# Attention, expert layer and MLP on one core: inputs laid out in chunks on the host, scores on halves of the array's rows, scalings on GpSimd

## The chip, the cores and the metric

The kernel runs on one core of one Trainium2 chip. The metric is the device time of one execution in microseconds (us).

## The reference

Three stages follow each other. The attention is a retention: scores are multiplied by a causal decay, without a softmax. Its output is the input of a layer that gives each token to one of eight experts, with a capacity, and the result goes through an MLP with x * sigmoid(1.702 x).

```python
# q, k, v: (4, 8, 576, 64) = batch, heads, positions, width; float32
scores = scale * np.matmul(q, k.transpose(0, 1, 3, 2))
gamma = 1.0 - 2.0 ** (-5.0 - np.arange(H))
Dmat = np.where(rel >= 0, gamma[:, None, None] ** rel[None, :, :], 0.0)
x = np.matmul(scores * Dmat[None], v)            # then to (2304, 512)
# experts: 8, w1 (8, 512, 1024), w2 (8, 1024, 512)
expert_idx = np.argmax(x @ w_gate, axis=1)       # weight: that expert's softmax
h = np.maximum(np.einsum('ecd,edf->ecf', disp, w1), 0.0)
y = np.einsum('ecf,efd->ecd', h, w2)             # rows back to their tokens, by weight
# MLP: w_in (512, 2048), w_out (2048, 512), given as float64
h = x @ w_in
g = h * (1.0 / (1.0 + np.exp(-1.702 * h)))
out = g @ w_out
```

## The kernel before

The change lies in the attention stage, the first 150 us. Its work is cut into 20 chunks (`NT`): each of the four batch rows has four chunks of 128 positions and one of 64 (`NC = 5`, `CH`). One chunk holds all eight heads, two of them beside each other in the 128 partitions, so that four pairs (`NP = 4`) make a tile of 128 x 4 x 128.

The decay gamma^(i-j) is split in a factor for the query's position (table `gq`) and one for the value's (`gv`); what is left for the scores is a causal mask (`mk`). The table `gq` is loaded for the first chunk of a batch row and scaled up by `scales(c)` on ScalarE (L303) for the others.

These functions emit the work of chunk n:

- `load(n)` (L261): three loads on SyncE's queue, of queries, keys and values, as rows of positions. Each head's 64 numbers are a piece of 256 bytes in the source (L268).
- `emit_T(n)` (L308): TensorE transposes the queries (L315) and keys (L321) in four pieces each. VectorE multiplies the turned queries by the decay on the way out of PSUM (L317); ScalarE copies the turned keys into `kz` (L324), a pair of tiles in which the rows of the other head of a pair are zeros.
- `emit_V(n)` (L326): VectorE multiplies the values by their decay (L331).
- `emit_SC(n)` (L334): eight score products, each over all 128 rows of the array, with `kz` as weights (L342). VectorE multiplies by the mask (L344).
- `emit_KV(n)` (L348): eight products of keys and values (L357) add up the state of a batch row; ScalarE copies it to `St` (L361). Each product fills one half of the array's columns.
- `emit_XO(n)` (L363): the output, from the state of the earlier chunks (L369) and the chunk's own scores (L372, by halves of the array's columns).
- `emit_XR(n)` (L377): the output of chunk n once more as rows and the routing scores of its tokens (L383), then three small steps on VectorE (L392 to L394).
- `emit_EX(n)`, `emit_ST(n)` (L397, L407): the weight of the chosen expert, and the weighted rows, stored in `xd`.
- `gate1`, `gate2`, `gate3`: for groups of chunks (`GROUPS`), lists of the tokens of each expert, mostly on VectorE.

An fp32 product or transpose in the program may be more than one instruction: the eight products of L342 are sixteen instructions of the trace.

The order is written out by hand in the loop over chunks (L555 to L595), and each engine works through its instructions in that order. Iteration n loads chunk n+4, turns chunk n+2, forms the scores of chunk n+1 and the output of chunk n, and the routing scores of chunk n-1:

```python
            load(n + 4)
            if n > 1:
                emit_T(n + 2)
            if n > 1:
                emit_ST(n - 2)
            emit_SC(n + 1)
            emit_XO(n)
            emit_KV(n + 1)
            if n:
                emit_XR(n - 1)
            emit_V(n + 2)
```

Other work is put between. The MLP's weights come as float64 and are rounded to float32 by `convert` (L204) in pieces of six VectorE steps (L216 to L224), with a load and, for some, a store on SyncE's queue. `pad()` puts such steps between VectorE's work for a chunk: `FILL_A` gives the number for each chunk of a batch row, `CONV_A` the pieces done in the attention stage, and `FILL_C` the number of steps by expert and step in the experts' stage, where the rest of them goes. GpSimd sets the tile `yh` to zero at the start (L290) and is then idle until it gathers the tokens of the first expert (L646). The first weights of an expert are loaded on SyncE's queue in the last iterations.

Of the kernel before, what the change touches and what calls it, by code (L numbers as in the profile page):

```python
# [11 lines left out]
F32 = mybir.dt.float32  # L12
# [10 lines left out]
P = 128  # L23
# [8 lines left out]
ZROW = N  # L32
GW = P + E
WR = [370, 344, 324, 314, 304, 294, 288, 278]
W = max(WR)
NB = N // P + E
# [8 lines left out]
CONV_A = 10  # L45
FILL_A = [4, 2, 4, 4, 4]
FILL_C = [0, 3, 3, 3, 3, 3, 3, 2]
# [7 lines left out]
def _consts():  # L55
    """Tables that depend on the shapes alone."""
# [10 lines left out]
    tri = (i[:, None] < i[None, :]).astype(np.float64)  # L67
# [10 lines left out]
    parts = [("ident", np.eye(P)), ("gq", gq), ("causal", causal), ("gv", gv), ("gs", gs), ("tri", tri),  # L78
# [16 lines left out]
def fused(ctx: ExitStack, tc, q, k, v, wg, w1, w2, cap, w_in, w_out, cf, out):  # L95
# [14 lines left out]
    # tables and state that live through the kernel  # L110
# [42 lines left out]
    def load_w(r, i):  # L153
        """An eighth of the weights for a place."""
# [20 lines left out]
    # ------------------------------------------------------------ float64 weights to float32  # L175
# [28 lines left out]
    def convert(lo, hi):  # L204
        """Rounds pieces of the weights to the nearest float32, from the words of the float64; an operation at a time."""
# [27 lines left out]
    # ------------------------------------------------------------ attention and routing  # L233
    with ExitStack() as a:
# [14 lines left out]
        tri_f = acst.tile([P, P], F32, name="tri_f")  # L249
        tri = acst.tile([P, P], BF16, name="tri")  # L250
        one = acst.tile([P, P], BF16, name="one")
        kz = [acst.tile([P, 2, NP, P], F32, name=f"kz{i}") for i in range(2)]
        St = [acst.tile([P, NP, P], F32, name=f"St{i}") for i in range(3)]

        qr, kr, vr = {}, {}, {}
# [5 lines left out]
        def load(n, *between):  # L261
            if n >= NT:
                return
            b, c = divmod(n, NC)
            C = CH[c]
            for nm, src, dst, bufs in (("q", q, qr, 3), ("k", k, kr, 4), ("v", v, vr, 5)):
                t = rows.tile([P, H, D], F32, tag=nm, name=nm, bufs=bufs)
                nc.sync.dma_start(t[:C], src[b, :, c * P:c * P + C, :].rearrange("h p d -> p h d"))  # L268
                dst[n] = t
                for f in between[:1]:  # L270
                    f()
                between = between[1:]

        load(0, lambda: (nc.sync.dma_start(ident, cc("ident")),
                         nc.sync.dma_start(gs, cc("gs").rearrange("p (c a) -> p c a", a=NP)),
                         nc.sync.dma_start(gq[:, 0], cc("gq").rearrange("p (a i) -> p a i", i=P))),
             lambda: nc.sync.dma_start(mk, cc("causal")))
        nc.sync.dma_start(gv, cc("gv").rearrange("p (c h) -> p c h", h=H))
        load(1)
        nc.sync.dma_start(iw[:, :, P:], wg.rearrange("(k p) e -> p k e", p=P))  # L280
        load(2)
        for i in range(2):
            nc.vector.memset(kz[i], 0.0)
# [6 lines left out]
        nc.gpsimd.memset(yh.bitcast(F32), 0.0)  # L290
        nc.gpsimd.dma_start(xd[ZROW:ZROW + 1, :], yh[0:1, 0, :DM].bitcast(F32))
# [13 lines left out]
        qT, at_t, xT_t, lg_t, kv_t, xr_t = {}, {}, {}, {}, {}, {}  # L305
# [20 lines left out]
        def emit_V(n):  # L326
            if n >= NT:
                return
# [719 lines left out]
```

## Time and profile before

| | us |
|---|---|
| median of 3 runs | 801.19 (798.92 to 801.2) |
| span of the profiled execution | 799.6 |
| TensorE busy | 768.2 (96%) |
| VectorE busy | 525.6 (66%) |
| ScalarE busy | 371.7 (46%) |
| GpSimd busy | 63.7 (8%) |

The profile is of one execution of its own, and its page gives the span from the first to the last instruction, 799.6 us. The busy shares are means over three stages with different limits: attention to about 150 us, the experts to about 505 us, then the MLP. PE is TensorE's products, PEld its loads of weights, DVE is VectorE, ACT ScalarE, POOL GpSimd and SP SyncE. Matmul ends are modelled, so the start of one group of products and the start of the next is a safer measure than the durations.

### The profile page before, as it was taken

How to read it: one execution, taken by the hardware profiler on the slowest of the kernel's cores; microseconds unless marked ns; L12 is line 12 of the kernel's file. 1: busy time of each engine (PE TensorE's matmuls, PEld its weight loads, DVE VectorE, ACT ScalarE, POOL GpSimd, SP SyncE). 2: the span in 40 equal slices, each digit the busy share in tenths (PEclk: the TensorE clock that was granted, in tenths of full speed). 3: DMA queues.
4: the chain of work that ended last, by engine and by line, in shares of the span. 5: the costliest groups of instructions: out<-in, count | busy, mean ns of one | idle time of the engine just before them, and what ended most of it. 6: DMA issues, size and time to landing. Idle time of an engine off the chain costs nothing.

```text
span 799.6 us, 13741 instructions
## 1 busy us (share of the span) xinstructions
PE 768.2 (96%) x5072; PEld 707.1 (88%) x5072; DVE 525.6 (66%) x1285; ACT 371.7 (46%) x788; POOL 63.7 (8%) x71
## 2 busy tenths in 40 slices
PE   6999996699999999999999999999999999999995
PEld 5899996689999999999999999999999988888884
DVE  3587888576787888898798888744434345343442
ACT  3655554336555566566544444444333344343432
POOL 5000000701011011000000000030000003000003
PEclk9999999699999999999999999999999999999998
DMA  9889858435576576675522222020000002000002
GB/s 196 193 195 223 199 126 282 128 107 181 175 251 199 195 245 204 195 268 169 202 67 66 67 67 66 1 80 1 1 0 1 1 1 80 0 1 1 1 1 82
DMA packets 94295, 90.26 MB, mean 113 GB/s; under 512 B 61719, under 2 KB 67223, under 8 KB 94224
## 3 DMA queue, kind: packets, MB, share of 16 engines
q1 hardware_dynamic: 77200, 45.90, 21.7%
q10 hardware_dynamic: 13312, 33.56, 13.1%
q0 software_dynamic: 3712, 9.88, 3.6%
q8 instruction: 42, 0.69, 0.4%
q14 instruction: 29, 0.24, 0.1%
HBM read 75.15 MB, written 14.16 MB: 112 GB/s over the span
## 4 chain that ended last, share of the span: by engine, by line
PE 60%; issue 31%; DVE 3%; POOL 2%; DMA 2%; ACT 1%; SPq 0%; POOLq 0%; ACTq 0%
PE h L674 14%; PE acc L693 13%; PE h L846 9%; PE y L871 8%; PE sc L342 4%; PE xr L383 2%; PE xo L372 2%; POOL out L884 2%; PE xo L369 2%; PE tx L654 1%; PE kv L357 1%; PE pk L321 1%; PE pq L315 1%; DMA xg<-xd,IDX 1%; DMA k<-in_k 0%
## 5 line engine op out<-in xcount | busy, mean ns | idle before, releaser
L852 DVE TENSOR_TENSOR sg<-h,sg 128x384 f32<-128x384 f32 (+1 forms) x96 | 53.5, 557 | 131.0 <-ACT sg L851 131.0
L851 ACT ACTIVATE sg<-h 128x384 f32<-128x384 f32 (+1 forms) x96 | 47.3, 492 | 165.1 <-PE h L846 163.9
L871 PE MATMUL y<-b,gh 128*128 128x512 f32 x288 | 112.4, 390 | 0.0
L871 PE MATMUL y<-a,gl 128*128 128x512 f32 x288 | 112.3, 390 | 0.0
L871 PE MATMUL y<-a,gh 128*128 128x512 f32 x288 | 112.2, 389 | 0.0
L625 DVE TENSOR_TENSOR b<-w1r,a 128x512 fp32r<-128x512 f32 x112 | 77.2, 689 | 14.8 <-ACT a L624 14.4
L846 PE MATMUL h<-yh,b 128*128 128x384 f32 (+2 forms) x384 | 82.7, 337 | 0.0
L846 PE MATMUL h<-yh,a 128*128 128x384 f32 (+2 forms) x384 | 82.7, 337 | 0.0
L846 PE MATMUL h<-yl,a 128*128 128x384 f32 (+2 forms) x384 | 82.6, 337 | 0.0
L854 ACT CAST gh<-sg 128x384 fp32r<-128x384 f32 (+1 forms) x96 | 49.3, 513 | 71.2 <-DVE sg L852 70.6
L693 PE MATMUL acc<-hi,a 128*128 128x370 f32 (+7 forms) x256 | 80.1, 313 | 0.0
L855 DVE TENSOR_TENSOR gl<-sg,gh 128x384 fp32r<-128x384 f32 (+1 forms) x96 | 53.6, 558 | 38.9 <-ACT gh L854 31.3
L693 PE MATMUL acc<-lo,a 128*128 128x370 f32 (+7 forms) x256 | 78.8, 308 | 0.0
L693 PE MATMUL acc<-hi,b 128*128 128x370 f32 (+7 forms) x256 | 78.8, 308 | 0.0
L634 DVE TENSOR_TENSOR b<-w2r,a 128x512 fp32r<-128x512 f32 x112 | 76.8, 685 | 1.8 <-ACT a L633 1.1
L633 ACT CAST a<-w2r 128x512 fp32r<-128x512 f32 x112 | 69.0, 616 | 17.7 <-PE acc L693 16.8
L846 PEld LDWEIGHTS h<-yh,a 128*128 128x128 f32 x384 | 68.2, 188 | 9.1 <-ACT yh L698 0.2
L624 ACT CAST a<-w1r 128x512 fp32r<-128x512 f32 x112 | 69.2, 618 | 12.6 <-issue 3.7
L846 PEld LDWEIGHTS h<-yh,b 128*128 128x128 f32 x384 | 66.4, 188 | 2.7
L846 PEld LDWEIGHTS h<-yl,a 128*128 128x128 f32 x384 | 66.1, 188 | 2.8
L871 PEld LDWEIGHTS y<-a,gl 128*128 128x128 f32 x288 | 54.1, 188 | 11.5
L871 PEld LDWEIGHTS y<-a,gh 128*128 128x128 f32 x288 | 54.1, 188 | 8.6
(157 smaller groups left out, 1305.0 us busy)
## 6 DMA issues: line engine op xcount, KB each, us to landing
w1r<-in_moe_w ACTq DMA_DIRECT2D x28, 512.0 KB, 4.4
w2r<-in_moe_w ACTq DMA_DIRECT2D x28, 512.0 KB, 3.6
cs<-in_moe_w_in SPq DMA_DIRECT2D x32, 256.0 KB, 3.2
cs<-in_moe_w_out SPq DMA_DIRECT2D x32, 256.0 KB, 2.7
q<-in_q SPq DMA_DIRECT2D x16, 256.0 KB, 3.9
k<-in_k SPq DMA_DIRECT2D x16, 256.0 KB, 4.6
v<-in_v SPq DMA_DIRECT2D x16, 256.0 KB, 4.8
xd<-xrow SPq DMA_DIRECT2D x16, 256.0 KB, 2.5
```

The lines of the kernel that those rows point to most:

```text
L624: nc.scalar.copy(a, s)
L625: nc.vector.tensor_tensor(b, s, a, op=ALU.subtract)
L633: nc.scalar.copy(a, s)
L634: nc.vector.tensor_tensor(b, s, a, op=ALU.subtract)
L674: nc.tensor.matmul(h[:, :n], wt[:, kc, :], xs[e, kc][j][:, :n], start=i == 0, stop=i == 3 * KC - 1)
L693: nc.tensor.matmul(y[dc][:, :n], wt[:, dc * P:(dc + 1) * P], x[:, :n], start=fc == 0 and i == 0, stop=fc == NF - 1 and i == 2)
L846: nc.tensor.matmul(h[:, :n], wt[:, kc, :], x[:, kc, o:o + n], start=i == 0, stop=i == 3 * KC - 1)
L851: nc.scalar.activation(sg[:, :n], h[:, :n], AF.Sigmoid, scale=1.702)
L852: nc.vector.tensor_tensor(sg[:, :n], h[:, :n], sg[:, :n], op=ALU.mult)
L854: nc.scalar.copy(gh[:, :n], sg[:, :n])
L855: nc.vector.tensor_tensor(gl[:, :n], sg[:, :n], gh[:, :n], op=ALU.subtract)
L871: nc.tensor.matmul(accs[bi][c // P + t], x[:, t * P:(t + 1) * P], wt, start=f == 0 and i == 0, stop=f == 2 * NF - 1 and i == 2)
```

## The change

Queries, keys and values are laid out by chunks before the launch (`_chunks`). `in_qk` has for each chunk 128 partitions with the queries and then the keys, already turned; `in_kv` has the keys and values as rows of positions. So `load(n)` is two loads, each with up to 4 KB in one piece for a partition, and the keys are loaded in both forms. The transposes, their evacuations, `kz` and its zeros go. Queries and values are multiplied by their decays in place, by `emit_Q(n)`, on GpSimd, and on VectorE for chunk 0 alone. Each score product uses 64 rows of the array, the upper or lower half, for one head of a pair.

Smaller parts: the products of the state (`emit_KV`) stand inside `emit_XO`, between the two kinds of output products, whose order is exchanged. All `scales` are made ahead of the loop. The zeros of `yh` are set in eight slices, in iterations 2 to 9. The table `tri` is made from two others. Six pieces of weights instead of ten are converted in the attention stage, two steps in each of iterations 2 to 17; the four others are added in the experts' stage.

```diff
+YW = (N + WR[1]) // 2
-CONV_A = 10
-FILL_A = [4, 2, 4, 4, 4]
-FILL_C = [0, 3, 3, 3, 3, 3, 3, 2]
+CONV_A = 6
+FILL_A = [2, 2, 2, 2, 2]
+FILL_C = [0, 3, 3, 3, 3, 4, 4, 3]
...
         def load(n, *between):
...
-            for nm, src, dst, bufs in (("q", q, qr, 3), ("k", k, kr, 4), ("v", v, vr, 5)):
-                t = rows.tile([P, H, D], F32, tag=nm, name=nm, bufs=bufs)
-                nc.sync.dma_start(t[:C], src[b, :, c * P:c * P + C, :].rearrange("h p d -> p h d"))
-                dst[n] = t
...
+            t = rows.tile([P, 2 * DM], F32, tag="qk", name="qk", bufs=5)[:, :2 * NP * C]
+            nc.sync.dma_start(t, qk[n, :, :2 * NP * C])
...
+            qT[n], kT[n] = t.rearrange("p (t a i) -> t p a i", t=2, a=NP)
+            t = rows.tile([P, 2, H, D], F32, tag="kv", name="kv", bufs=5)
+            nc.sync.dma_start(t[:C].rearrange("p t h d -> p (t h d)"), kv[n, :C, :])
+            kr[n], vr[n] = t[:, 0], t[:, 1]
...
-        nc.gpsimd.memset(yh.bitcast(F32), 0.0)
-        nc.gpsimd.dma_start(xd[ZROW:ZROW + 1, :], yh[0:1, 0, :DM].bitcast(F32))
...
-        def emit_T(n):
...
-        def emit_V(n):
...
+        def emit_Q(n, g=nc.gpsimd):
...
+            g.tensor_tensor(qT[n], qT[n], gq[:, c, :, :C], op=ALU.mult)
+            g.tensor_tensor(vr[n][:C], vr[n][:C], gv[:C, c, :, None].to_broadcast([C, H, D]), op=ALU.mult)
...
         def emit_SC(n):
...
-                    nc.tensor.matmul(sc[:C, hh, p, :C], kz[n % 2][:, hh, p, :C], qT[n][:, p, :C], start=True, stop=True)
+                    r = slice(D * hh, D * hh + D)
+                    nc.tensor.matmul(sc[:C, hh, p, :C], kT[n][r, p, :], qT[n][r, p, :], start=True, stop=True)
...
         def emit_XO(n):
...
             for p in range(NP):
-                if c:
-                    nc.tensor.matmul(xo[:, p, :C], St[n % 3][:, p, :], qT[n][:, p, :C], start=p == 0, stop=False, skip_group_check=True)
-            for p in range(NP):
                 for hh in range(2):
                     nc.tensor.matmul(xo[D * hh:D * hh + D, p, :C], vr[n][:C, 2 * p + hh, :], at_t[n][:C, NP * hh + p, :C],
-                                     start=not c and p == 0, stop=p == NP - 1, skip_group_check=True)
+                                     start=p == 0, stop=not c and p == NP - 1, skip_group_check=True)
+            emit_KV(n + 1)
+            for p in range(NP):
+                if c:
+                    nc.tensor.matmul(xo[:, p, :C], St[n % 3][:, p, :], qT[n][:, p, :], start=False, stop=p == NP - 1, skip_group_check=True)
...
-        emit_T(0)
-        emit_V(0)
+        emit_Q(0, nc.vector)
         emit_SC(0)
         emit_KV(0)
         load(3)
-        scales(1)
-        emit_T(1)
-        scales(2)
-        emit_V(1)
+        for c in range(1, NC):
+            scales(c)
+        emit_Q(1)
...
+            emit_Q(n + 2)
+            if 1 < n < 10:
+                nc.gpsimd.memset(yh[:, (n - 2) // 2, (n % 2) * YW:(n % 2 + 1) * YW].bitcast(F32), 0.0)
+            if n == 10:
+                nc.gpsimd.dma_start(xd[ZROW:ZROW + 1, :], yh[0:1, 0, :DM].bitcast(F32))
             emit_SC(n + 1)
...
-            emit_KV(n + 1)
...
-            emit_V(n + 2)
...
+def _chunks(q, k, v):
+
+    qk = np.zeros((NT, P, 2 * DM), np.float32)
+    kv = np.zeros((NT, P, 2 * DM), np.float32)
+    turned = [a.reshape(B, NP, 2, S, D).transpose(0, 2, 4, 1, 3).reshape(B, P, NP, S) for a in (q, k)]
+    rows = [a.transpose(0, 2, 1, 3).reshape(B, S, DM) for a in (k, v)]
+    for n in range(NT):
+        b, c = divmod(n, NC)
+        C, s = CH[c], slice(c * P, c * P + CH[c])
+        qk[n, :, :2 * NP * C] = np.stack([a[b, :, :, s] for a in turned], 1).reshape(P, 2 * NP * C)
+        kv[n, :C] = np.concatenate([a[b, s] for a in rows], 1)
+    return qk, kv
```

The order on TensorE, from the output of chunk 5 to the routing scores of chunk 5, before; the line numbers are those of the kernel before:

```order
L369 MATMUL xo<-qT,St_123 128x128 x4
L372 MATMUL xo<-at,v 64x128 x8
L357 MATMUL kv<-v,k 64x64 x8
L383 MATMUL xr<-iw,xT 128x136 x4
L315 MATMUL pq<-ident,q 128x64 x4
L321 MATMUL pk<-ident,k 128x64 x4
L342 MATMUL sc<-qT,kz_121 128x128 x8
L369 MATMUL xo<-qT,St_124 128x128 x4
L372 MATMUL xo<-at,v 64x128 x8
L357 MATMUL kv<-v,k 64x64 x8
L383 MATMUL xr<-iw,xT 128x136 x4
```

The same place after the change, with the line numbers of the changed kernel (L348 are the outputs from the chunk's own scores, L336 the state, L353 the outputs from the state, L363 the routing scores, L321 the scores):

```order
L348 MATMUL xo<-at,kv 64x128 x8
L336 MATMUL kv<-kv 64x64 x8
L353 MATMUL xo<-qk,St_120 128x128 x4
L363 MATMUL xr<-iw,xT 128x136 x4
L321 MATMUL sc<-qk 128x128 x8
L348 MATMUL xo<-at,kv 64x128 x8
L336 MATMUL kv<-kv 64x64 x8
L353 MATMUL xo<-qk,St_121 128x128 x4
L363 MATMUL xr<-iw,xT 128x136 x4
```

The transposes are gone from between the routing scores and the next chunk's scores, and the outputs from the state stand behind the products of the next state.

GpSimd's order before, from the small memsets of the start to the gathers of the first expert:

```order
L289 MEMSET acc 128x24
L290 MEMSET yh 128x10592
L291 DMA xd<-yh 16x1x32
L646 DMA xg<-xd,IDX_70 128x512 x2
L646 DMA xg<-xd,IDX_70 114x512
```

After, from the same memset on, the first chunks (L309 scales queries, L310 values, L552 is a slice of the zeros):

```order
L286 MEMSET acc 128x24
L309 ISA
L309 TENSOR_TENSOR qk<-qk,gq 128x512
L310 TENSOR_TENSOR kv<-kv,gv 128x512
L309 TENSOR_TENSOR qk<-qk,gq 128x512
L310 TENSOR_TENSOR kv<-kv,gv 128x512
L309 TENSOR_TENSOR qk<-qk,gq 128x512
L310 TENSOR_TENSOR kv<-kv,gv 128x512
L309 TENSOR_TENSOR qk<-qk,gq 128x256
L310 TENSOR_TENSOR kv<-kv,gv 64x512
L552 MEMSET yh 128x1324
```

Two multiplications for each chunk stand on GpSimd, and an eighth of the zeros behind those of chunks 4 to 11.

## Rows read from the trace of the kernel before

**Rows 1.** The page's 40 slices of 20 us, busy share in tenths.

```profile
PE   6999996699999999999999999999999999999995
PEclk9999999699999999999999999999999999999998
```

**Rows 2.** Stretches by stage: length, busy us of engines, clock, transfer share, GB/s.

```profile
0.00:30.00 30.00, 21.23 (x176) 18.70 (x176) 12.35 (x22) 12.45 (x29) 10.08 (x10) 0.94 1.00 189
30.00:125.00 95.00, 94.88 (x1135) 89.07 (x1134) 76.65 (x265) 54.63 (x137) 0.00 (x0) 1.00 0.82 197
125.00:150.00 25.00, 12.51 (x112) 9.89 (x110) 16.26 (x85) 7.22 (x20) 5.50 (x6) 0.73 0.64 207
...
412.00:452.00 40.00, 40.00 (x204) 36.49 (x204) 34.78 (x87) 18.13 (x40) 0.00 (x0) 1.00 0.22 66
```

The columns after the length are PE, PEld, DVE, ACT and POOL.

**Rows 3.** The same view: two batch rows, and a stretch with weight loads.

```profile
60.35:89.19 28.84, 28.84 (x350) 27.14 (x348) 23.32 (x79) 16.55 (x41) 0.00 (x0) 1.00 0.87 201
89.19:118.79 29.60, 29.49 (x352) 27.59 (x352) 23.79 (x85) 16.54 (x41) 0.00 (x0) 1.00 0.69 162
120.00:130.00 10.00, 9.70 (x116) 8.86 (x115) 7.66 (x27) 4.99 (x15) 0.00 (x0) 1.00 0.97 338
```

**Rows 4.** Chain of waits in the batch row 60.35 to 89.19, by line.

```profile
by line: PE sc L342 28.8%; PE xr L383 18.8%; PE xo L372 16.3%; PE xo L369 13.9%; PE pq L315 7.9%; PE kv L357 7.0%; PE pk L321 6.9%; PE ix L521 0.8%; PE pr L477 0.4%; PE pr L474 0.3%; PE pr L472 0.1%
```

**Rows 5.** Chain of waits in order of time: start, length in us, what.

```profile
2.79 3.72 DMA k<-in_k
...
8.34 3.96 PE sc L342 x16
...
16.31 3.47 PE sc L342 x16
...
30.99 1.98 PE sc L342 x16
...
66.24 1.07 PE sc L342 x16
...
73.43 1.04 PE xo L369 x8
...
76.82 0.44 PE pq L315 x4
...
77.69 1.79 PE sc L342 x16
79.48 1.02 PE xo L372 x16
80.50 0.47 PE kv L357 x16
...
124.28 1.09 PE sc L342 x16
...
149.55 1.03 PE h L674 x2
```

**Rows 6.** Groups by line: GpSimd's, and VectorE's of the batch row.

```profile
L290 POOL MEMSET yh<- 128x10592 f32 x1 | 8.9, 8921 | 0.0
...
L286 POOL MEMSET one<- 128x128 bf16 x1 | 0.2, 205 | 0.3 <-POOLq L1028 0.3
...
L331 DVE TENSOR_TENSOR v<-v,gv 128x512 f32<-128x512 f32 (+1 forms) x5 | 3.4, 681 | 0.0
L317 DVE TENSOR_TENSOR qT<-pq,gq 128x512 f32<-128x512 f32 (+1 forms) x5 | 3.1, 617 | 0.0
L217 DVE SCALAR_TENSOR_TENSOR cu<-cs,cu 128x256 int32<-128x256 int32 x3 | 1.2, 417 | 0.0
```

Each row ends with busy us and mean ns of one, then the idle time before it.

**Rows 7.** DMA queues (packets, MB, share of 16 engines), and one kind of load.

```profile
q1 hardware_dynamic: 77200, 45.90, 21.7%
q10 hardware_dynamic: 13312, 33.56, 13.1%
...
w1r<-in_moe_w ACTq DMA_DIRECT2D x28, 512.0 KB, 4.4
```

The load's last number is the median us from issue to landing.

More of the change, by code (lines that the diff above doesn't have):

```diff
@@ L77, in _consts @@
     tw = np.broadcast_to((np.array(WR)[:, None] + P * np.arange(NR)[None, :])[None], (P, E, NR))
-    parts = [("ident", np.eye(P)), ("gq", gq), ("causal", causal), ("gv", gv), ("gs", gs), ("tri", tri),
+    parts = [("ident", np.eye(P)), ("gq", gq), ("causal", causal), ("gv", gv), ("gs", gs),
              ("ca", ca), ("cb", cb), ("ids", ids), ("idz", ids - ZROW), ("idp", np.stack([ids // 16, ids % 16], 2)),
@@ L94, in fused @@
 @with_exitstack
-def fused(ctx: ExitStack, tc, q, k, v, wg, w1, w2, cap, w_in, w_out, cf, out):
+def fused(ctx: ExitStack, tc, qk, kv, wg, w1, w2, cap, w_in, w_out, cf, out):
     nc = tc.nc
@@ L248, in fused @@
         iw = acst.tile([P, KC, GW], F32, name="iw")
-        tri_f = acst.tile([P, P], F32, name="tri_f")
         tri = acst.tile([P, P], BF16, name="tri")
         one = acst.tile([P, P], BF16, name="one")
-        kz = [acst.tile([P, 2, NP, P], F32, name=f"kz{i}") for i in range(2)]
         St = [acst.tile([P, NP, P], F32, name=f"St{i}") for i in range(3)]
-        qr, kr, vr = {}, {}, {}
+        qT, kT, kr, vr = {}, {}, {}, {}
         def cc(name):
@@ L263, in load @@
                 return
-            b, c = divmod(n, NC)
-            C = CH[c]
-            for nm, src, dst, bufs in (("q", q, qr, 3), ("k", k, kr, 4), ("v", v, vr, 5)):
-                t = rows.tile([P, H, D], F32, tag=nm, name=nm, bufs=bufs)
-                nc.sync.dma_start(t[:C], src[b, :, c * P:c * P + C, :].rearrange("h p d -> p h d"))
-                dst[n] = t
[L270 to L277, printed above, removed]
+            C = CH[n % NC]
+            t = rows.tile([P, 2 * DM], F32, tag="qk", name="qk", bufs=5)[:, :2 * NP * C]
+            nc.sync.dma_start(t, qk[n, :, :2 * NP * C])
+            for f in between:
+                f()
+            qT[n], kT[n] = t.rearrange("p (t a i) -> t p a i", t=2, a=NP)
+            t = rows.tile([P, 2, H, D], F32, tag="kv", name="kv", bufs=5)
+            nc.sync.dma_start(t[:C].rearrange("p t h d -> p (t h d)"), kv[n, :C, :])
+            kr[n], vr[n] = t[:, 0], t[:, 1]
+        load(0, lambda: (nc.sync.dma_start(gq[:, 0], cc("gq").rearrange("p (a i) -> p a i", i=P)),
+                         nc.sync.dma_start(mk, cc("causal"))))
         nc.sync.dma_start(gv, cc("gv").rearrange("p (c h) -> p c h", h=H))
         load(1)
+        nc.sync.dma_start(gs, cc("gs").rearrange("p (c a) -> p c a", a=NP))
+        nc.sync.dma_start(ident, cc("ident"))
         nc.sync.dma_start(iw[:, :, P:], wg.rearrange("(k p) e -> p k e", p=P))
         load(2)
-        for i in range(2):
-            nc.vector.memset(kz[i], 0.0)
         for i in range(3):
@@ L557, in fused @@
             extra = FILL_A[c] if 1 < n < NT - 2 else 0
-            plan[:] = [extra * (i + 1) // 4 - extra * i // 4 for i in range(4)]
+            plan[:] = [extra * (i + 1) // 2 - extra * i // 2 for i in range(2)]
             load(n + 4)
@@ L584, in fused @@
                 gate2(ends[n - 1])
-            emit_KV(n + 1)
-            if n < 2:
-                emit_T(n + 2)
-                scales(n + 3)
             if n:
                 emit_XR(n - 1)
-            emit_V(n + 2)
             if n in ends:
@@ L1033, in give @@
         args.append(nc.dram_tensor(name, a.shape, mybir.dt.from_np(a.dtype), kind="ExternalInput").ap())
+    qk, kv = _chunks(*(np.asarray(inputs[x]) for x in "qkv"))
+    give("in_qk", qk)
+    give("in_kv", kv)
     for name in _INS:
```

32 lines of the change are left out of this document (5 added, 27 removed).

## The prediction, made before the change was run

> **What bounds the kernel now.** I read four views in this order: the forty slices of the page, busy time by stage, the chain of waits in order of time, and the groups by line of the engines that receive or lose work.
>
> The slices show TensorE busy in nearly every tenth of the span, except at about 120 to 160 us, where its clock also falls [rows 1]. By stage [rows 2], TensorE is busy 94.88 of 95 us between 30 and 125 us, the attention stage in its steady part, at a granted clock of 1.00, while VectorE has 76.65 and GpSimd nothing. So a microsecond of TensorE work taken out there is a microsecond of time, until another engine or the transfers take over. From 125 to 150 us the chain runs through VectorE, a store and the first gather; from there to the end TensorE bounds again, on work that the change does not touch.
>
> Inside the stage I take one batch row of five chunks as the unit: 28.84 us, from score to score, with TensorE busy throughout; the one after it took 29.60 [rows 3]. Of its chain [rows 4] the transposes of queries and keys (L315, L321) are 7.9% and 6.9%, together 4.27 us, and the scores (L342) 28.8%, 8.31 us. One chunk of the chain [rows 5] shows prices: four transposes 0.44, the scores' sixteen instructions 1.79, the sixteen of L372, whose outputs lie in halves of the array's columns, 1.02, the sixteen of L357 0.47. Full-array work therefore goes at 112 ns an instruction, and work by column halves at 64, or 128 a pair: the halves run together.
>
> From the score products of chunk 3 (30.99) to those of chunk 19 (124.28) are 93.3 us [rows 5], 5.83 a chunk.
>
> **The change part by part.** My sum runs over three stretches: up to chunk 3's scores, from there to chunk 19's, and the rest.
>
> *Transposes gone.* 4.27 us a batch row, all on the path. Their evacuations go too: L324 on ScalarE, which is not near its limit, and the multiplication L317 is moved.
>
> *Scores by row halves.* The same sixteen instructions, each on 64 rows of the array. No row shows two row halves at once. The near row is L372 [rows 5]: a pair of column halves needs 128 ns where one full instruction needs 112, so 1.02 for sixteen. That is one bound, 8.31 becoming about 4.8. The other bound is no gain: the loads of the weights might not overlap. For this speaks that L369 takes 1.04 even in the chunk with only 64 moving columns [rows 5], so there the load of 128 weight columns sets the pace, and row halves load 128 columns each, column halves only 64. Against it: L357 loads 64 columns sixteen times in 0.47, while full-height scores with 64 weight columns take 1.07 for the same number [rows 5]; loads into separate parts of the array do overlap. I take the gain, 3.5 us a batch row, and leave a quarter of the chance to the other.
>
> TensorE then needs 28.84 - 4.27 - 3.5 = 21.1 us a batch row, 4.2 a chunk.
>
> *VectorE.* It has 23.3 us in the batch row [rows 3]. It loses five scalings of queries and five of values (617 and 681 ns [rows 6]), 6.5 us, and of 18 conversion steps 8, at some 0.37 (L217 is the longest kind, 417 ns), 3.0 us. 13.8 of 21.1 are left. That hides, but not evenly: once in five chunks it also builds the lists of a group, before it looks at the routing scores that the next L383 needs. This already shows in the batch row that took 0.76 us longer. With a chunk of 4.2 instead of 5.8 us I take twice that, 1.5 a batch row or 0.3 a chunk. So 4.5 a chunk.
>
> *GpSimd.* It gets two multiplications of 128x512 a chunk and, in eight chunks, an eighth of the memset of yh. The memset is 8921 ns for 10592 elements [rows 6], 0.84 ns each, so 1.12 us a slice. Of a two-input operation on GpSimd no row exists. Lower bound: the memset's rate, 0.43 us. Upper: the small memset L286 has 1.6 ns an element with its fixed cost, and three such streams give 2.5 us. I take three streams at the large memset's rate, 1.29, nearer in size. Then a chunk costs GpSimd 2.6 us, 3.7 with its slice, under 4.5: hidden. It also has an iteration of lead, for it scales chunk n+2 in iteration n. At the upper bound it would be 4.9 and 6.0; over a batch, with its half chunk, about 5.6 a chunk in the eight with a slice and 4.5 later, some 9 us more in all. From the page alone (the Trainium skill, GPSIMD Engine Reference, "Performance versus the Vector engine") the estimate would be 1.1 us an operation, and the sum stays the same.
>
> *Transfers.* Three loads a chunk in pieces of 256 bytes become two with 4 KB a partition, and keys come twice: 14.2 MB become 18.9. The queue with larger packets moved 33.56 MB in 13.1% of the span, 320 GB/s, the mixed one 45.90 MB in 21.7%, 265 [rows 7]; a stretch with weight loads shows 338 at a share of 0.97 [rows 3]. Up to chunk 19's scores some 22.5 MB moved, from the rates of [rows 2] less the weights at the end; 4.7 more, and 1.6 less for four conversion pieces, make 25.6 MB, 76 us at 338. That is under the 93 us at which I expect to stand there, but no longer far under. SyncE issues two loads instead of three, and behind each the stores and conversion loads wait as before. Hidden.
>
> *Order within a chunk.* The state products (L357) go ahead of those with St: no work is added, St has been ready for an iteration. Zero.
>
> *The start.* Before, the scores of chunk 0 begin at 8.34, those of chunk 1 at 16.31, chunk 3's at 30.99 [rows 5], held by loads (one sits in the chain for 3.72), by transposes and by slow first products (3.96 for sixteen, later 1.79). After: 0.75 MB of queries, keys and decay table land at about 5.5 (512 KB took 4.4 from issue [rows 7]), one scaling on VectorE, scores from 6.2 for about 2.0, the state, its copy, the decay tables of chunk 1 (1.3), GpSimd 1.3: scores of chunk 1 at about 13. Two chunks of some 3.8 to 4.6 us follow: chunk 3 at 21.5, 9.5 earlier. The large memset no longer stands before GpSimd's work.
>
> *Steady part.* 16 x 4.5 = 72 against 93.3: 21.3 saved.
>
> *The rest.* From 124.28 to the first expert product at 149.55 [rows 5] nothing leaves the chain but one scaling, and four conversion steps instead of two are pushed in: zero. The 24 conversion steps moved to the experts cost VectorE 8.9 us where it has 34.8 of 40 us busy [rows 2] at the fullest; spread over three experts they hide behind TensorE. If they did not: up to 8.9.
>
> **Sum.** 799.6 - 9.5 - 21.3 = 768.8 of span. The runs' median is 801.19, 1.6 above this span, so **770 us**.
>
> **The rivals.**
>
> *Row halves don't overlap.* TensorE keeps 3.5 us a batch row: 5.2 a chunk, 11 us more in the steady part and 1 at the start, **782**. Evidence for and against stands above.
>
> *VectorE and GpSimd block each other.* GpSimd's ten operations a batch row would each hold back one of VectorE's for their whole length: 13.8 + 11.6 = 25.4 us, 5.1 a chunk, TensorE waiting for the masked scores and the routing; **780**. No stretch of this trace has both at work on inputs, so no row speaks for or against it. The Trainium skill states such a rule (SBUF — State Buffer, "SBUF: two separate sides"): a VectorE operation with two inputs in SBUF and a GpSimd operation that reads SBUF exclude each other for the whole instruction. By that rule the conversion and list steps would be held, the masks, whose scores lie in PSUM, not directly, and the time would move from 770 towards this rival's 780.
>
> *The transfers bind.* If the large pieces moved no faster than attention's mean (197 GB/s at a share of 0.82 [rows 2], 240 when full), 25.6 MB need 107 us: chunk 19 is 14 later than forecast, **784**. Against it: rows 7.
>
> *GpSimd is much slower than its memsets.* Then it sets the pace. The point that decides: from chunk 1's scores to chunk 19's before were 108 us, 6.0 a chunk, and the start gives 3; GpSimd needs 1.8 operations a chunk on the mean and 0.5 of memset, so from about 3.1 us an operation the change is slower. At 4 us, 7.7 a chunk, **some 830**. It would take over three times the row I start from.
>
> **How the numbers follow.** Forecast, with VectorE's stalls between none (765) and double (775): 0.55. Row halves serial: 0.18. Blocking: 0.14. Transfers: 0.08. Slow GpSimd: 0.05, nearly all of it slower. A measurement here tells 0.3%, 2.4 us, from no change. Only in the last case could the time be within or above that: faster 0.94, same 0.02, slower 0.04. For the range I go down to 757, the smooth case with a start 3 us better still and a few us off my prices, and up to 787, which takes in serial halves, blocking and slow transfers, but not two of them together.
>
> **What would show it.** Scores at about 1.0 us a chunk in the chain, not 1.8; chunks 4.2 to 4.7 apart; GpSimd operations near 1.3 us; a transfer share of 0.9 or more with over 300 GB/s; chunk 19's scores near 93 us; unchanged times from there on. I am wrong if TensorE's chain is broken by waits for GpSimd or loads, if VectorE's conversion steps grow well over 417 ns beside GpSimd, or if the experts take longer than before.

## The result, and the profile after

The changed kernel took **788.03 us** in the median of 4 runs (786.94 to 792.42), the kernel before 801.2 beside it: a ratio of 0.9853 with a 95% interval of 0.9824 to 0.9881. It is faster, by 13 us where 31 were forecast, and stands 1 us above the range. The profiled execution, the fastest of the four (786.94 us), has a span of 785.1 us, 16.3 above the 768.8 of the sum.

The page: the busy line, and TensorE's slices, which answer to [rows 1].

```profile
PE 737.1 (94%) x4912; PEld 675.7 (86%) x4912; DVE 517.0 (66%) x1245; ACT 350.3 (45%) x748; POOL 106.1 (14%) x116
...
PE   4788983999999999999999999999999999999995
```

TensorE lost 31 us of work (768.2 before), the size of the forecast gain. But the second to sixth slices, which were full before, stand at 7 to 9: more than half of it came back as idle time.

The stretches by stage that answer to [rows 2] and [rows 3] (columns as there). The first row runs from chunk 3's scores to chunk 19's, the last from score to score of one batch row.

```profile
23.66:107.83 84.17, 71.94 (x993) 64.86 (x993) 65.94 (x204) 34.64 (x96) 41.05 (x37) 0.98 0.71 238
28.00:36.00 8.00, 4.17 (x42) 3.55 (x41) 3.48 (x14) 2.64 (x7) 2.40 (x3) 0.79 0.87 288
59.43:84.18 24.75, 22.15 (x312) 19.86 (x311) 20.56 (x64) 10.78 (x31) 10.93 (x12) 1.00 0.80 271
```

A batch row takes 24.75 us, where it took 28.84 and the forecast had 22.6. No engine is full in it, and the transfers are at a share of 0.80. So the kernel is bounded there by a chain that passes from engine to engine. Between 28 and 36 us half the time is lost; there the mean granted clock falls to 0.79, so part of that stretch ran at the lower level, 1.2 GHz.

TensorE's timeline (start, length, line, idle before in brackets) of chunks 1, 3 and 4, of the outputs behind chunk 3's scores, of chunk 19's scores and of the first expert product:

```profile
13.98 2.08 PE L321 MATMUL sc<-qk 64*128 64x128 f32 x16 [3.52 <-POOL qk L309]
...
23.66 1.16 PE L321 MATMUL sc<-qk 64*128 64x128 f32 x16
24.75 1.09 PE L348 MATMUL xo<-at,kv 128*64 128x128 f32 x16
...
32.19 1.12 PE L321 MATMUL sc<-qk 64*64 64x64 f32 x16 [3.83 <-DVE at L323]
...
107.83 0.68 PE L321 MATMUL sc<-qk 64*64 64x64 f32 x16
...
134.23 1.79 PE L649 MATMUL h<-xh,a 128*128 128x370 f32 x4
```

These answer to [rows 5] and split the 16.3 us. Chunk 3's scores start at 23.66, 2.2 later than forecast. From there to chunk 19 are 84.2 us instead of 72, 12.2 more. From chunk 19 to the first expert product are 26.4 instead of 25.3, 1.1 more, and what follows takes 0.8 more. The scores themselves are as forecast: sixteen instructions in 1.09 us (23.66 to 24.75).

The waits between 20 and 110 us (who, for what, us in total, times, longest):

```profile
POOL qk L309 <- DMA qk<-in_qk: 27.4, 12, 5.6
...
PE sc L321 <- DVE at L323: 4.5, 2, 3.8
...
DVE cu L216 <- DMA cs<-in_moe_w_in: 4.1, 1, 4.1
...
PE pr L452 <- DVE mx L384: 3.9, 3, 1.4
...
PE xr L363 <- ACT xrow L393: 3.7, 6, 1.2
```

TensorE waits in three places: for masked scores (twice, one wait of 3.8 us), three times for the lists of a group (`pr`), and six times in front of the routing scores (`xr`), whose PSUM tile ScalarE has not yet read out into `xrow`. Together these are 12.1 us, about what TensorE idles between chunk 3's scores and chunk 19's (84.17 less 71.94). No row of TensorE's in this list names GpSimd or a load: GpSimd itself waits for its loads, and it is not late as a supplier.

Groups by line: VectorE between 30 and 100 us, which answers to [rows 6].

```profile
L323 DVE TENSOR_TENSOR at<-sc,mk 128x512 f32<-128x512 f32 (+1 forms) x29 | 18.0, 619 | 0.0
L374 DVE TENSOR_SCALAR lg<-lg,mx 128x8 f32<-128x8 f32 (+1 forms) x14 | 9.2, 660 | 0.6
...
L217 DVE SCALAR_TENSOR_TENSOR cu<-cs,cu 128x256 int32<-128x256 int32 x5 | 3.1, 614 | 0.0
...
L471 DVE TENSOR_TENSOR ge<-RO,sml 128x10 f32<-128x10 f32 x2 | 1.7, 866 | 0.1
```

And GpSimd's groups over the whole span:

```profile
L309 POOL TENSOR_TENSOR qk<-qk,gq 128x512 f32<-128x512 f32 x15 | 19.1, 1273 | 39.2 <-DMA qk<-in_qk 25.8 <-ACT gq L298 11.6 <-PE xr L363 1.8
...
L310 POOL TENSOR_TENSOR kv<-kv,gv 128x512 f32<-128x512 f32 x15 | 16.7, 1112 | 2.5 <-DMA kv<-in_kv 2.5
```

GpSimd's price is the forecast one (1273 and 1112 ns against 1290). On VectorE, L374 subtracts a maximum from 128 x 8 numbers. It takes 660 ns on the mean in this stretch. The view of one line (least, median and most ns of all 20) gives for the same step in the kernel before, and then in the changed one:

```profile
L394 DVE TENSOR_SCALAR lg<-lg,mx x20: 223/231/235, 30.6 to 134.6; 128x8 f32<-128x8 f32 x16, 64x8 f32<-64x8 f32 x4
```

```profile
L374 DVE TENSOR_SCALAR lg<-lg,mx x20: 223/340/1652, 24.2 to 118.0; 128x8 f32<-128x8 f32 x16, 64x8 f32<-64x8 f32 x4
```

The timeline shows that this is no cost of the step itself:

```profile
59.41 1.20 POOL L552 MEMSET yh<- 128x1324 f32 x1
...
60.09 0.56 DVE L374 TENSOR_SCALAR lg<-lg,mx 128x8 f32<-128x8 f32 x1
...
63.64 1.27 POOL L309 TENSOR_TENSOR qk<-qk,gq 128x512 f32<-128x512 f32 x1 [3.03 <-DMA qk<-in_qk]
...
63.90 1.03 DVE L374 TENSOR_SCALAR lg<-lg,mx 128x8 f32<-128x8 f32 x1
...
68.56 1.33 DVE L374 TENSOR_SCALAR lg<-lg,mx 128x8 f32<-128x8 f32 x1
68.60 1.26 POOL L309 TENSOR_TENSOR qk<-qk,gq 128x512 f32<-128x512 f32 x1 [2.05 <-DMA qk<-in_qk]
...
70.51 0.16 DVE L385 RECIPROCAL mx<-mx 128x1 f32<-128x1 f32 x1
...
70.76 0.69 ACT L393 ACTIVATE xrow<-xr,mx 128x512 f32<-128x512 f32 x1 [0.47 <-PE kv L336]
...
71.50 0.68 PE L363 MATMUL xr<-iw,xT 128*64 128x136 f32 x4 [0.81 <-ACT xrow L393]
```

Add start and length: GpSimd's instructions end at 60.61, 64.91 and 69.86, the three L374 at 60.65, 64.93 and 69.89. Each time the small step ends with GpSimd's instruction, whenever it began. All twenty of them fit: twelve have a GpSimd instruction beside them and end 0.01 to 0.04 us after the end of one, and the eight with none beside them take 0.22 or 0.23 us. The last three lines show who pays: the exponential and the reciprocal stand behind L374, `xrow` behind the reciprocal, and the next routing scores behind `xrow`. (The bracket of `xrow` names products of TensorE that end at about the same moment; in the program `xrow` reads the reciprocal and the routing scores' tile only.)

### The profile page after: what moved, and what is told of

Its sections match the earlier page's. It is cut to its first block, busy times and chain, and to the rows that moved or that the text cites. A ratio compares the mean times of both kernels' runs of the same rounds, so it can differ in the third digit from the quotient of the medians.

```text
span 785.1 us, 13394 instructions
## 1 busy us (share of the span) xinstructions
PE 737.1 (94%) x4912; PEld 675.7 (86%) x4912; DVE 517.0 (66%) x1245; ACT 350.3 (45%) x748; POOL 106.1 (14%) x116
## 4 chain that ended last, share of the span: by engine, by line
PE 46%; issue 32%; DVE 4%; POOL 3%; DMA 1%; ACT 0%; POOLq 0%; ACTq 0%; DVEq 0%
PE acc L668 13%; PE h L649 13%; PE h L821 9%; PE y L846 8%; POOL out L859 2%; PE tx L629 1%; DMA xg<-xd,IDX 1%; DVE b L609 0%; DVE lo L654 0%; DMA cs<-in_moe_w_in 0%; DVE b L600 0%; PE xr L363 0%; POOL xg L621 0%; PE acc L725 0%; DVE ct L697 0%
## 5 line engine op out<-in xcount | busy, mean ns | idle before, releaser
L668 PE MATMUL acc<-hi,a 128*128 128x370 f32 (+7 forms) x256 | 80.1, 313 | 0.0
L859 POOL DMA_INDIRECT out<-ob,PERM x18 | 17.8, 991 | 435.0 <-ACT ob L856 431.7
```

The lines of the kernel that those rows point to most:

```text
L668: nc.tensor.matmul(y[dc][:, :n], wt[:, dc * P:(dc + 1) * P], x[:, :n], start=fc == 0 and i == 0, stop=fc == NF - 1 and i == 2)
```

## The experiments

My theory after these readings had two causes: GpSimd's work holds VectorE's steps, and conversion loads come too late. In the expectations A is the case for this theory, B the case against it. Each ratio is to the kernel before, measured beside it, with its 95% interval.

**The loads.** `conv_load(0)` and `(1)` stood in iteration 1 and now stand in iteration 3, but the first conversion step is still emitted in iteration 2, ahead of a mask, and issues its loads itself, at 27.52. The timeline of the changed kernel:

```profile
27.52 1.39 SPq L202 DMA_DIRECT2D cs<-in_moe_w_in  x3
...
31.04 0.29 DVE L216 TENSOR_SCALAR cu<-cs 128x256 int32<-128x256 int32 x1 [4.12 <-DMA cs<-in_moe_w_in]
31.25 0.68 DVE L323 TENSOR_TENSOR at<-sc,mk 128x512 f32<-128x512 f32 x1
```

Experiment e1 puts the two loads back:

```diff
             if n == 1:
...
+                conv_load(0)
+                conv_load(1)
             if n == 3:
...
-                conv_load(0)
-                conv_load(1)
```

> The changed kernel with the first two conversion loads issued in iteration 1 again, as before the change, and not by the first conversion step that needs them. Theory A (the late load holds up VectorE for 4.1 us, TensorE for 3.8, and TensorE's clock falls after it): the wait goes, chunk 4's scores come about 4 us earlier, chunk 19's by 4.5 to 6, and the time falls by 4.5 to 6, to about 782. Rival B (the stage is held by VectorE's chain at large and catches up): chunk 4's scores come earlier, chunk 19's by less than 2, time less than 2 us lower.

783.99 us, ratio 0.9791 [0.9771, 0.9811], 4.0 us less than the changed kernel, a little short of A's 4.5; chunk 4's scores start at 27.80 instead of 32.19, chunk 19's at 102.18, 5.65 earlier. The same windows as above:

```profile
22.99:102.18 79.19, 70.60 (x994) 63.58 (x993) 65.62 (x204) 34.95 (x96) 40.82 (x37) 1.00 0.74 247
28.00:36.00 8.00, 6.82 (x103) 6.00 (x100) 6.37 (x19) 3.32 (x10) 4.60 (x5) 1.00 0.97 318
```

The trace is as A had it: the hole of 28 to 36 us is gone, and the clock stays at full speed there. The waits in front of the routing scores (4.5 us) and of the lists (3.4) stay: they have another cause.

**GpSimd's work taken away.** e2 leaves out the scaling of queries and values of chunks 1 to 19. The routing differs by it, so only the attention stage is read. With nothing ahead of them, the zeros of `yh` are set at the start too (1.0 to 10.2 us): GpSimd then rests until the gathers.

```diff
-            if n >= NT:
+            if n >= NT or n:
                 return
```

> The changed kernel without the multiplications by the decays on GpSimd: queries and values of chunks 1 to 19 are left unscaled, so the routing and what follows it differ; read only the attention stage in its profile. Theory A (GpSimd's multiplications hold back VectorE's steps): the step that subtracts the largest routing score (L374, 660 ns on the mean in the stretch 30 to 100 us of the changed kernel) is back at 230, the conversion steps of L217 and L222 at 415, and TensorE's 12.2 us of waits between the scores of chunk 3 and chunk 19 fall by 5 or more, the one wait of 3.8 for the conversion load staying. Rival B (the waits come from the order of the instructions): the durations may fall, the waits by less than 2.

One run, 773.68 us; span 771.8. Windows from chunk 3 to chunk 19, and of a batch row; then VectorE's groups between 30 and 96 us:

```profile
20.55:93.65 73.10, 68.89 (x993) 63.01 (x992) 51.61 (x204) 35.34 (x96) 0.00 (x0) 1.00 0.82 281
49.37:71.10 21.73, 21.40 (x312) 19.63 (x311) 15.91 (x63) 11.14 (x30) 0.00 (x0) 1.00 0.89 307
```

```profile
L323 DVE TENSOR_TENSOR at<-sc,mk 128x512 f32<-128x512 f32 (+1 forms) x29 | 18.2, 629 | 0.0
L374 DVE TENSOR_SCALAR lg<-lg,mx 128x8 f32<-128x8 f32 (+1 forms) x15 | 3.4, 229 | 0.5
...
L217 DVE SCALAR_TENSOR_TENSOR cu<-cs,cu 128x256 int32<-128x256 int32 x5 | 2.1, 411 | 0.0
...
L471 DVE TENSOR_TENSOR ge<-RO,sml 128x10 f32<-128x10 f32 x3 | 0.5, 170 | 0.1
```

VectorE's same 204 instructions take 51.61 us instead of 65.94: 14.3 us were holding. L374 is back at 229 ns, the conversion step L217 at 411; the masks, which read PSUM, never changed. The steady part shortens by 11.1 us (84.2 to 73.1), though VectorE still waits 4.2 us for the late load there, and TensorE 2.6 with it; of the 11.1, 9.8 lie behind that load, from chunk 4's scores to chunk 19's (75.6 us in the changed kernel, 65.8 here, 27.83 to 93.65). A batch row takes 21.73 us, where my sum had 22.6. This is A.

**The same work on VectorE.** e5 keeps the scalings and moves them.

```diff
-        def emit_Q(n, g=nc.gpsimd):
+        def emit_Q(n, g=nc.vector):
```

> The changed kernel with all scalings of queries and values on VectorE, none on GpSimd. VectorE gets 1.3 us of work more a chunk and is held back by nobody. Theory A (being held back costs VectorE, and TensorE behind it, about what the work itself would cost): from chunk 3's scores to chunk 19's 78 to 85 us where the changed kernel has 84.2, the time within 4 us of 788, L374 at 230 ns. Rival B (GpSimd relieves VectorE at a small price): over 88 us there, the time 793 or more.

783.33 us, 0.9782 [0.9761, 0.9802]: 4.7 us faster than with GpSimd doing the work, a little beyond what theory A allowed.

```profile
21.95:104.67 82.72, 71.30 (x994) 64.58 (x993) 68.99 (x236) 35.68 (x96) 0.00 (x0) 0.98 0.74 242
```

VectorE carries 32 more instructions between the same two scores (236 for 204) and is busy only 3.05 us longer. What GpSimd took off it, GpSimd's holding gave back almost entirely. The steady part is 1.45 us shorter than the changed kernel's, so the same work costs a little less on VectorE. It is not the whole gain: of the 3.8 us by which e5's span is shorter (781.3), 1.7 come before chunk 3's scores (21.95 for 23.66) and 0.9 between chunk 19's scores and the first expert product; 0.3 go back behind it. As in e2, the zeros of `yh` are set at the start.

**The step that is held on the path.** e6 removes L374: the maximum is kept negated and given to the exponential as its bias, and added once for a group in `gate1`.

```diff
-            nc.vector.tensor_reduce(mx[:C, 0:1], lg, op=ALU.max, axis=AX.X)
-            nc.vector.tensor_scalar(lg, lg, mx[:C, 0:1], None, op0=ALU.subtract)
+            nc.vector.tensor_reduce(nm_t[g][:C, c0:c0 + 1], lg, op=ALU.max, axis=AX.X, negate=True)
...
-            nc.scalar.activation(ex[:C], lg_t[g][:C, c0, :], AF.Exp, accum_out=mx[:C, 1:2])
+            nc.scalar.activation(ex[:C], lg_t[g][:C, c0, :], AF.Exp, bias=nm_t[g][:C, c0:c0 + 1], accum_out=mx[:C, 1:2])
```

> The changed kernel without the step that subtracts the largest routing score for each chunk (L374): the largest is kept negated, goes into the exponential as its bias, and is subtracted once for a group. Theory A (this step, held back by GpSimd, is what delays the weighted rows and so the routing products): TensorE's waits for the weighted rows, 3.9 us between chunk 3 and chunk 19, fall below 1.5, and the time falls by 3 to 5. Rival B (the next VectorE steps are held back in its place): the time falls by less than 1.5.

783.16 us, 0.977 [0.9748, 0.9792], 4.9 us less than the changed kernel, as A had it; the steady part 80.1 us (23.99 to 104.13). The waits of `xr` for `xrow` fall to 1.0 us. The run takes the step's own 0.23 us out of the chain together with the time that it is held, and does not part the two. Some of the holding moved to other steps: one of the conversion steps takes 709 ns on the mean between 30 and 100 us, where the changed kernel has 361:

```profile
L216 DVE TENSOR_SCALAR cu<-cs 128x256 int32<-128x256 int32 x5 | 3.5, 709 | 4.8 <-DMA cs<-in_moe_w_in 4.8
```

**Row halves alone.** e3 is the kernel before with the scores by row halves; the keys leave PSUM in one piece and the zeros of `kz` go.

```diff
-                    nc.tensor.matmul(sc[:C, hh, p, :C], kz[n % 2][:, hh, p, :C], qT[n][:, p, :C],
+                    r = slice(D * hh, D * hh + D)
+                    nc.tensor.matmul(sc[:C, hh, p, :C], kz[n % 2][r, p, :C], qT[n][r, p, :C],
```

> The kernel before with one part of the change alone: scores by halves of the array's rows, the turned keys copied without zeros in one piece. Theory A (in the kernel before, TensorE's own work is the bound of the attention stage): sixteen score instructions take 1.09 us instead of 1.79, a batch row loses about 3.1 us of 28.8, and the time falls by 10 to 13 us, to 788 to 791. Rival B (VectorE's chain stands right behind TensorE's): half of it or less, 795 or more.

791.32 us, 0.9885 [0.9867, 0.9902]: 9.9 us less, just under what theory A expected. The profiled run is the slowest of the five, 794.48. A chunk's scores and a step of VectorE's in the chain behind them, from the chain of waits:

```profile
67.28 1.09 PE sc L339 x16
...
72.54 0.23 DVE lg L391
```

The sixteen instructions take 1.09 us here too, so the halves do run together. The batch row from 62.48 to 88.91 shrinks by 2.4 us and not by 3.5, since the chain now passes through VectorE. That the total is near A's comes of several parts, read in that run: chunk 3's scores come 6.0 us earlier (24.95), which A did not have; VectorE then waits 5.2 us once for a conversion load, and chunk 4's scores come only 0.9 earlier; from there to chunk 19's are 79.6 us instead of 86.9, 7.3 less.

**Lists later.** e4 emits `gate2` and the expert's first loads behind the outputs in every group.

```diff
-            if n - 1 in ends and n < NT - 1:
-                gate2(ends[n - 1])
...
             emit_XO(n)
-            if n - 1 in ends and n == NT - 1:
+            if n - 1 in ends:
                 gate2(ends[n - 1])
```

> The changed kernel with the lists of a group emitted after the outputs of the same iteration in place of ahead of them, and the first weight loads behind them. Theory A (TensorE waits 1.2 to 1.4 us, three times between chunk 3 and chunk 19, at the counting products L452 for the choice of experts): these waits go and nothing takes their place: 3 to 4 us less, about 784.5. Rival B (VectorE is what is late, and only TensorE's place of waiting moves): the routing products wait longer for the weighted rows instead, and the time falls by less than 1.5 us.

789.64 us, 0.9874 [0.9851, 0.9897]: no gain over the changed kernel. The waits of `pr` are gone, but `xr` now waits 6.3 us for `xrow` instead of 3.7. B came out: the delay changed its place.

**The start.** e7 loads `gs` ahead of `gv` and of chunk 1's data, and makes the decay table of chunk 1 before the state of chunk 0, whose copies held ScalarE.

```diff
+        scales(1)
         emit_KV(0)
         load(3)
-        for c in range(1, NC):
+        for c in range(2, NC):
             scales(c)
```

> The changed kernel with the small table gs loaded ahead of the values' table, and the decay tables of chunk 1 made before the first copies of the state on ScalarE. Theory A (chunk 1's scores wait for GpSimd, GpSimd for the table of chunk 1, and that for the copies of the state): chunk 1's scores come at about 11.5 in place of 13.98, the time falls by 1.5 to 2.5. Rival B (the gain is lost in the wait for the conversion load): chunk 1's scores come earlier, chunk 4's not, less than 0.8 in the time.

786.15 us, 0.9819 [0.9788, 0.985], an interval that overlaps that of the changed kernel: unclear by time (the medians differ by 1.9, which A allowed and B did not). The trace is plain: chunk 1's scores come at 11.81, 2.2 earlier, chunk 3's at 21.42, 2.2 earlier, and chunk 4's at 32.52, no earlier than in the changed kernel (32.19). The late load swallows it, as B had it.

**The decay on the other side.** The outputs are linear in the queries, so e9 multiplies them by `gq` on their way out of PSUM; GpSimd keeps the values alone.

```diff
-            g.tensor_tensor(qT[n], qT[n], gq[:, c, :, :C], op=ALU.mult)
...
-            nc.scalar.copy(xT_t[n][:, :, :C], xo[:, :, :C])
+            nc.vector.tensor_tensor(xT_t[n][:, :, :C], xo[:, :, :C], gq[:, c, :, :C], op=ALU.mult)
```

> The changed kernel with the queries' decay applied to the outputs: VectorE multiplies by the table on the way out of PSUM, where ScalarE copied (L355), and GpSimd scales the values alone. VectorE has 0.6 us more a chunk, reading one operand from PSUM; GpSimd reads half as long. Theory A (VectorE is held back by GpSimd's reading, not by its own load): L374 under 450 ns on the mean, chunk 1's scores at about 10.5, from chunk 3's scores to chunk 19's some 80 us, the time 5 to 9 us lower, 779 to 783. Rival B (VectorE's own work is what is short): the steady part gets no shorter, the time falls by less than 3, which the start gives.

784.04 us, 0.9799 [0.9775, 0.9823], 4.0 less than the changed kernel, between A's 5 and B's 3. Chunk 3 comes at 19.18, 4.5 earlier, for the first scores wait for no scaling; the steady part is 86.3, longer than the 84.2, which is B. The 2.1 us more are the late load again, which comes no earlier with the scores: chunk 4's scores are at 29.73, and from there to chunk 19's are 75.8 us against 75.6. With half of GpSimd's multiplications the subtraction takes 441 ns, as A had it, but TensorE now waits 4.1 us for the outputs that VectorE brings out of PSUM.

**Together.** e8 joins e1, e6 and e7, and gives VectorE twelve conversion steps a batch row (`FILL_A = [3, 2, 2, 3, 2]`). e10 is e1, e6, e7 and these steps with e9's edit; e11 is e8 with e5's edit; e12 is e11 with e9's edit and the values' scaling behind the masks, without e7's moves.

> The changed kernel, scalings still on GpSimd, with the early conversion loads, without the step for the largest score, with the start's two moves, and with all 36 conversion steps spread over iterations 2 to 17, none left to be done in one piece at the end. Theory A (conversion load, held-back steps and start are separate losses, each met once): the single gains of 4.0, 4.9 and 1.9 us add up to most of their sum, 776 to 779. Rival B (behind each lies the same chain, VectorE held back by GpSimd): little more than the best of them, 781 or more.

> As e8_all, with the queries' decay applied to the outputs on VectorE, so that GpSimd reads for the values alone. Theory A (less reading on GpSimd, less holding back): 2 to 4 us under e8_all. Rival B (VectorE is full): the same or slower.

> As e8_all, with all scalings on VectorE and none on GpSimd. Theory A (GpSimd's two operations a chunk cost VectorE at least the time that they save it, so they bring nothing in the best arrangement either): at or below e8_all, 774 to 778. Rival B (once the blocked step is gone from the chain, GpSimd is the better place): 3 or more above e8_all.

> As e11_vector_all, with the queries' decay applied to the outputs on VectorE, in place of ScalarE's copy, and the values scaled behind the masks. VectorE has as much work as in e11_vector_all, but the scores wait for the loads alone. Theory A (in e11_vector_all the scores wait for VectorE's scaling ahead of them): another 1 to 4 us less, 772 to 776; chunk 1's scores under 10 us. Rival B (VectorE's sum is the bound, whatever the order): within 1 us of e11_vector_all.

| | us | ratio to before |
|---|---|---|
| e8 | 779.28 | 0.9743 [0.9726, 0.9760] |
| e10 | 778.96 | 0.9736 [0.9714, 0.9757] |
| e11 | 777.57 | 0.9728 [0.9715, 0.9741] |
| e12 | 777.68 | 0.9726 [0.9712, 0.9739] |

Most of the gains add: e1, e6 and e7 alone gave 4.0, 4.9 and 1.9 against the changed kernel's 788.03, 10.8 together, and e8 gives 8.75, just short of A. The kernel before took 799.83 us beside these four and 801.2 or 801.3 beside the others; counted from it, e8 has 7.4 of 10.9. What the twelve conversion steps a batch row do was not run alone. Chunk 3's scores come at 20.82 and chunk 4's at 25.42: with the load early, e7's 2.2 us survive. The four agree within their intervals; all beat both kernels, the best ones by 10 us against the changed kernel. e11 came out as its A: with all scalings on VectorE the kernel is no slower than e8, so GpSimd's multiplications bring nothing in this arrangement either. In e11:

```profile
30.00:90.00 60.00, 53.68 (x785) 48.67 (x784) 52.62 (x179) 28.91 (x76) 0.00 (x0) 1.00 0.77 258
```

TensorE and VectorE are each busy for some nine tenths of the time. Whether the decay is put on the queries or on the outputs makes no difference: B in e12 against e11, where VectorE does it either way, and in e10 against e8, where it moves from GpSimd to VectorE.

## Why the prediction was wrong

**The step that failed: "Then a chunk costs GpSimd 2.6 us, 3.7 with its slice, under 4.5: hidden."** I priced GpSimd's operations rightly and asked only whether they end in time. They do; they cost by what they stop meanwhile. That was the rival "VectorE and GpSimd block each other", with a chance of 0.14, and that VectorE is held is what e2 and e5 show: 14.3 us in its work, and with GpSimd's work gone the steady part is 11.1 us shorter. The sign that I had named came too: conversion steps well over 417 ns (614). The rival stood at 780, with 5.1 us a chunk; the steady part shows 5.26, of which the late load is 0.3. That these are so near is in part luck: the rival had 11.6 us of holding in a batch row and VectorE full, where the rows show 4.65 (20.56 less 15.91) and VectorE busy for 20.56 of 24.75. Less is held than the rival had, but on the path.

The rule that I had weighed there (the Trainium skill, SBUF — State Buffer, "SBUF: two separate sides") says that a VectorE operation with two inputs in SBUF and a GpSimd operation that reads SBUF exclude each other for the whole instruction. The trace agrees for the conversion steps (614 ns beside 411 without GpSimd) and the lists (866 beside 170), and the masks, with one input in PSUM, are not held (619 and 629). What I missed is that the step that mattered is none of these: L374, with one array of 128 x 8 as input, held to 660 ns and standing in the chain from one routing score to the next. The same section of the Trainium skill names a second case, VectorE in a mode that uses two ports, against any GpSimd operation; L374 behaves like it, and I had left that case out. I had looked for long steps instead of for steps on the path. That a port which the two engines share is the cause is the Trainium skill's reading; the runs show the holding, and that it goes with GpSimd's work.

**The step I did not price: the loads that moved.** I counted conversion steps pushed to the experts, and costed the loads as hidden; that `conv_load` went two iterations later while the first step stayed was in the change, though not among the lines of the diff shown ahead of the prediction. e1 puts it at 4.0 us, 5.0 of the span, counting the TensorE clock that fell with the hole.

**The steady part.** TensorE needs 4.3 us a chunk without GpSimd (68.89 by 16), for 4.2 forecast. e2's 73.1 less TensorE's 2.6 at the late load are 70.5, and its stretch behind that load, 65.8 for fifteen chunks, gives 70.2 for sixteen. So the 72 would have held without the holding and the late load, and its allowance of 4.8 for VectorE's stalls was enough; no run has the scalings on GpSimd without the holding.

**The start** was 2.2 us late, 1.0 up to chunk 1's scores (13.98 for the "about 13" forecast) and 1.2 in the two chunks behind. GpSimd waited for the decay table, which stood behind two copies on ScalarE:

```profile
10.51 0.76 ACT L340 COPY St<-kv 64x256 f32<-64x256 f32 x2 [7.20 <-PE kv L336]
...
12.67 1.26 POOL L309 TENSOR_TENSOR qk<-qk,gq 128x512 f32<-128x512 f32 x1 [11.60 <-ACT gq L298]
```

e7 gave 2.2 back by this order and the earlier load of `gs` together.

**The rest** was not zero: 1.1 us to the first expert product and 0.8 behind it. I had costed the four conversion steps there at nothing. They do stand on VectorE between a routing score's maximum and its reciprocal (108.50 to 110.16), but the rows do not put the 1.1 us down to them: the last routing scores come 7.0 us after chunk 19's, and came 7.1 after them before the change (124.28 in [rows 5]). The time is lost behind them. Two lines of the kernel before, then two of the changed one:

```profile
131.38 2.27 PE L383 MATMUL xr<-iw,xT 128*128 128x136 f32 x16 [0.32 <-ACT xrow L413]
...
135.78 1.26 ACT L413 ACTIVATE xrow<-xr,mx 128x512 f32<-128x512 f32 x2 [0.57 <-PE pr L477]
```

```profile
114.87 2.27 PE L363 MATMUL xr<-iw,xT 128*128 128x136 f32 x16 [0.42 <-ACT xrow L393]
...
121.35 0.68 ACT L393 ACTIVATE xrow<-xr,mx 64x512 f32<-64x512 f32 x1 [1.51 <-DMA xd<-xrow]
```

ScalarE wrote the rows of the last two chunks one right behind the other; now the second waits 1.5 us for an earlier store out of `xrow`, and the first gather, which reads what these stores write, starts 17.6 us after chunk 19's scores (125.43) instead of 16.2 (140.51). Two runs bear on it. e5 has the four steps, writes the two rows together again, and needs 25.5 us to the first expert product. e8 has none of the steps there: its last routing scores come 6.1 us after chunk 19's (98.47 and 104.57), and the first expert product still 26.6 (125.11), for the second row waits again. What makes the store late, and what the 0.8 us are, stays open.

**What held.** The row halves run together (1.09 us for sixteen, forecast 1.02), which ends the rival of serial halves (for its chance the prediction has a quarter in one place and 0.18 in another). GpSimd's price is within 14% of the row that I took. The transfers do not bind: a share of 0.80 in the batch row, and in e2 0.89 with 307 GB/s, though chunks there follow each other faster.

## What to carry to other kernels

An idle engine is not free if its work holds up the engine that it relieves: ask of every small step on the path what it would wait for when the helper works, for its own length (0.2 us) is then no measure of its cost. When steps or loads are moved, compare for each pair where the load is issued and where its first reader stands in its engine's order, and who is queued behind that reader. Once the bounding engine has less to do, the next bound is often a chain through several half-idle engines, and taking one step out of it can shorten it (e6, 4.9 us) where moving work to an idle engine does not: with the scalings back on VectorE the kernel was 4.7 us faster in e5, and no slower in e11.

## What was unexpected of the hardware

A VectorE step of 0.23 us on 128 x 8 numbers took up to 1.65 us, for it may be held by two GpSimd instructions in a row. In e7 it was four: one step from 21.95 to 25.80, while GpSimd's instructions ended at 22.41, 23.42, 24.56 and 25.78, three of them begun after the step. It is held by a memset as well, which reads no tensor: the first pair in the timeline of the changed kernel, the memset ending at 60.61 and the step at 60.65. The row of 24.19 us shows both:

```profile
23.42 1.03 POOL L310 TENSOR_TENSOR kv<-kv,gv 128x512 f32<-128x512 f32 x1
...
24.19 1.43 DVE L374 TENSOR_SCALAR lg<-lg,mx 128x8 f32<-128x8 f32 x1
24.40 1.19 POOL L552 MEMSET yh<- 128x1324 f32 x1
```

A multiplication that ends at 24.45 and a memset that ends at 25.59 lie over the step, which ends at 25.62. A step with two inputs was held otherwise. L224, a conversion step that adds two arrays in 0.41 us without GpSimd, began at 42.64 beside a multiplication and ended at 43.30, 0.28 behind the multiplication's end and inside a memset (42.96 to 44.16); the subtraction behind it began at 43.63 beside the same memset and ended with it, at 44.18.

The steps beside it that fold a row into one number, or treat one number a partition, were not longer than without GpSimd: the maximum (L373) took 160 ns in both, the reciprocal 162.
